# The end of attention and the start of the gated layer: a new plan of loads and preparing steps, part of it on GpSimd, and two tiles turned by TensorE

## The chip, the cores and the metric

The kernel runs on one core of a Trainium2 chip, as one program. The metric is the device time of one execution in microseconds. Before the change it is 778.28 us, the median of three runs (777.83 to 778.59).

## The reference, cut to what matters

Four batches of eight heads over 576 positions, head size 64; then a gated layer over the 2304 tokens, 512 wide inside and out, 1536 in the middle.

```python
scores = q @ k.T / sqrt(64) + bias                    # bias: a small network of the positions, per head
attn = exp(scores - max(scores)); attn = attn / (attn.sum(-1) + 1e-9)
x = (attn @ v)                                        # [4, 8, 576, 64] -> [2304, 512]
out = (sigmoid(x @ w_gate) * (x @ w_val)) @ w_out     # w_* come as float64 pairs of 32-bit words
```

## The kernel before, in words

It has three stages. The first builds the position bias (up to about 116 us). The second is attention, the third the gated layer (`Moe`).

**Attention.** There are 16 units, one for each pair of heads and batch, the batch running fastest: units 12 to 15 are the last pair of heads with batches 0 to 3. A unit has nine steps, numbered through as `n`; `score` (L633, L622) makes the scores `sc` on TensorE for two steps at a time, one for each head h, `soft` takes the bias and the row minimum on VectorE (L649) and the exponential on ScalarE (L654), which leaves `en`, 128 x 576. Two steps later `turn` (L673 to L686) transposes `en` into `at`, in two fp16 pieces, high and low. Head 0 and the ninth step go through TensorE: four 128 x 128 transposes into `pt`, the high piece on ScalarE, the low one on VectorE (`split`, L563, L564). The steps in `CROSS` (1, 3, 5, 7: all of head 1) go another way: GpSimd makes the two pieces `cr` (L531, L672), and a transposing DMA from SyncE's queue (L673) brings them into `at`, due `XLAG` = 2 steps later. `products` (L738) multiplies `at` with the values, in two halves of 14 pieces of two matmuls each, the second half of the columns after the first; `FILL` says how many pieces follow each step, and they belong to the unit before. After the last step two halves of the last unit remain. `tail` turns the ninth tile's last 64 columns, `normal` the row sums.

**Around the last units.** From unit 12 on, `extra(n)` runs at the end of each step and does what `PLAN` names, with n counted from unit 12's first step: `l0` loads 128 rows of `x` (piece 0 of four) of token chunk 0, `r0` the reciprocal sums of these rows, each `x0` is one of the steps of `prep_x` (nothing, the product with the reciprocals on VectorE, a high piece on ScalarE, a low piece on VectorE), `s` stages the next weight block from HBM, `w0` is the next step of weight block 0 (high piece on ScalarE, low piece on VectorE), `t` loads ScalarE's sigmoid table. Capital letters are chunk 1. What is left is done by `START[0]` ahead of the layer's first matmul, `START[1]` and `START[2]` behind the first and second pair. The order on an engine is not only that of the code: a scheduler may pull a step ahead, as the rows below show.

**The gated layer.** `ORDER` walks over pairs of a chunk (A: 0, B: 1) and one of 12 blocks of 128 middle columns: 24 matmuls of `gates` (L985) into `pg` and `pu`, then nine of `outs` (L1009) for the pair before. The blocks' weights are split into two pieces, those of blocks 3 and up also narrowed from float64, on VectorE and ScalarE, by `convert`, whose calls stand among the pairs. Engines run their instructions in order; SyncE's DMA queue too, so a load that waits holds those behind it.

Of the kernel before, what the change touches and what calls it, by code (L numbers as in the profile page):

```python
# [10 lines left out]
F32 = mybir.dt.float32  # L11
# [5 lines left out]
ALU = mybir.AluOpType  # L17
# [6 lines left out]
HF = S // 2  # L24
NCH = S // 64
FILL = (0, 7, 0, 7, 0, 7, 0, 7, 0)
ENB = 11
WM = 6
LAG, WSTEP, VSTEP, TAIL = 2, 2, (3, 5), 3
# [15 lines left out]
PRE = lambda f, z: f < 3  # L45
ORDER = "A0 A1 B0 A2 B1 A3 B2 A4 B3 A5 B4 A6 B5 A7 B6 A8 B7 A9 B8 A10 A11 B9 B10 B11"
CONV = (2, 1)
START = 'x0 x2 w3 x2 X0 s w0 w4 R1 w3 X0 w5 R2 X1 w4 w5 X2 w2 X1 L3 s X2 X1 X1', 'R3 s X2 s s X2 s', 'X3 X3 X3 X3'
PLAN = {
# [3 lines left out]
RAWS = 11  # L53
SLOTS = (12, 17)
ETILES, XTILES, XVARS = (7, 8), 10, 10
# [461 lines left out]
def attention(tc, att, q, k, v, biases, biasL, ident, xs, rs, sizes, extra):  # L517
# [41 lines left out]
    def half(ap):  # L559
        return ap.rearrange("p (a b) -> p a b", a=2)  # L560

    def split(hi, lo, ps):
        nc.scalar.activation(out=hi, in_=ps, func=AF.Copy, scale=float(2.0 ** UP))  # L563
        return lambda: nc.vector.scalar_tensor_tensor(out=lo, in0=ps, scalar=float(2.0 ** UP), in1=hi, op0=ALU.mult, op1=ALU.subtract)  # L564

    def pool_split(hi, lo, src):
        copy(hi, src)
# [90 lines left out]
    def turn(n):  # L658

        u, s = divmod(n, 9)  # L660
        p, b = units[u]
        if s == 0:
            state[u][1] = atp.tile([128, 2, 9, S], F16, name="at")
        sm, at, ens = state[u]
        h, it = TURN[s] if s < 8 else (0, 4)
        en = ens[4 * h + it if s < 8 else 8]
        i = slice(128 * it, 128 * it + 128)
        if s in CROSS:
            t = crp.tile([128, 2 * S], F16, name="cr")
            copy(t[:, 0:S], en)  # L670
            for a, z in ((640, slice(0, 512)), (S, slice(512, S))):
                nc.gpsimd.tensor_tensor(out=t[:, a:a + z.stop - z.start], in0=en[:, z], in1=t[:, z], op=ALU.subtract)  # L672
            crossed.append((n + LAG + XLAG, lambda: nc.sync.dma_start_transpose(out=at[:, h, :, i], in_=t)))  # L673
            return []
        after = []
        pt = ps_t.tile([128, 4, 128], F32, name="pt")
        for J in range(4):
            nc.tensor.transpose(pt[:, J], en[:, 128 * J:128 * J + 128], ident)  # L678
        if s == 8:
            return [split(at[:, h, 0:4, 512:576], at[:, h, 5:9, 512:576], pt[:, :, 64 * h:64 * h + 64]) for h in range(2)]  # L680
        after.append(split(at[:, h, 0:4, i], at[:, h, 5:9, i], pt))
        if it == 3:
            pt = ps_t.tile([128, 4, 128], F32, name="pt")
            for e in range(4):
                nc.tensor.transpose(pt[0:64, e], ens[4 * h + e][:, 512:576], ident)
            after.append(split(at[0:64, h, 4, 0:512], at[64:128, h, 4, 0:512], pt[0:64].rearrange("p e i -> p (e i)")))  # L686
        return after

    def tail(u):
# [60 lines left out]
    with tc.manual_schedule():  # L750
        work = iter(())
        after, late, due, loads = [], [], [], []
        for n in range(9 * NU + LAG + 1):
# [25 lines left out]
                inverse()  # L779
            if s == WSTEP and 0 < u < NU:  # L780
                work = products(u - 1)
            if n == 9 * NU + LAG - 1:
                work = products(u - 1)
            for _ in range(FILL[s] if n < 9 * NU else 14 if n < 9 * NU + LAG else 0):
                f = next(work, None)
                if f:
                    f()
# [3 lines left out]
                after.append(lower_v(u, VSTEP.index(s - 2)))  # L791
            if s == 8 and u + 1 < NU:
                loads.append(lambda z=u + 1: load_v(z))
            extra(n)
        for f in after + late:
            f()
        for f in work:
# [6 lines left out]
class Moe:  # L804
# [43 lines left out]

    def early(self, stack):

        self.open(stack, "right", sig=1, xin=3, xrec=2, x=4, wfirst=6)

    def ahead(self, n):
        self.do(PLAN.get(n, ""))
# [31 lines left out]

    def load_x(self, c, kc, eng=None):
        ts = slice(self.T * c, self.T * c + self.T)
        t = self.pools["xin"].tile([128, 2, self.T], F32, name="xin")
        (eng or self.nc.sync).dma_start(out=t[:, 0], in_=self.xs[128 * kc:128 * kc + 128, ts])  # L890
        return t

    def load_r(self, c, kc, eng=None):
# [5 lines left out]

    def prep_x(self, c, t, r, hi, lo, kc):  # L900
        nc = self.nc
        x = t[:, 0]

        return [lambda: None,
                lambda: nc.vector.tensor_tensor(out=x, in0=x, in1=r, op=ALU.mult),
                lambda: nc.scalar.activation(out=hi[:, kc], in_=x, func=AF.Copy),
                lambda: nc.vector.tensor_tensor(out=lo[:, kc], in0=x, in1=hi[:, kc].bitcast(F32), op=ALU.subtract)]

    def stage(self, eng=None):
        n = self.staged  # L910
# [12 lines left out]
    def begin(self):  # L923
# [11 lines left out]
        def upper():  # L935
            p = self.pools["wfirst" if n < 3 or (z == 2 and n > 5) else "wa"]
            t = p.tile([128, 2, 4, 128], F32R, tag="w", name=f"w{z}_{f}")
            self.wts[b] = t[:, 0], t[:, 1], t
            nc.scalar.activation(out=t[:, 0], in_=m, func=AF.Copy)
            if self.squares is None:  # L940
                self.unsized.append((f, z, t))
            else:
                self.size(f, z, t, t[:, 1])
# [70 lines left out]
    def store(self, c, t):  # L1014
        po = self.po.pop((c, t))
        if t == 2:
            ob = self.pools["xin"].tile([128, 2, self.T], F32, name="xin").rearrange("p s t -> p (s t)")[:, 0:DM]
        else:
            ob = self.pools["ob"].tile([128, DM], F32, name="ob")
        self.nc.scalar.activation(out=ob, in_=po, func=AF.Copy, **({"scale": self.un[c // 2][1]} if c > 1 else {}))  # L1020
# [335 lines left out]
```

## Time and profile before

| | us |
|---|---|
| runs, median (lowest to highest) | 778.28 (777.83 to 778.59) |
| the profiled execution, its own time | 779.37 |
| its span, first to last instruction | 777.6 |

| engine | busy us | share of the span |
|---|---|---|
| TensorE matmul (PE) | 729.3 | 94% |
| VectorE (DVE) | 632.7 | 81% |
| ScalarE (ACT) | 549.0 | 71% |
| GpSimd (POOL) | 325.3 | 42% |

Shares are means over stages that differ, so the stretches below are read one by one. Engines have the names in brackets, PEld is TensorE's weight load, SPq and ACTq are the DMA queues of SyncE and ScalarE. `x12` behind a name is a count. In a timeline row the brackets hold the time the engine was idle before the row and what ended it. PEclk is the share of full clock that TensorE was granted, 1.00 being 2.4 GHz.

### The profile page before, as it was taken

To read this page: it belongs to the slowest core of one execution; us is meant where nothing else is said; L and a number is where in the kernel's file an instruction comes from. 1 tells how busy PE (TensorE), PEld (TensorE's weight loads), DVE (VectorE), ACT (ScalarE), POOL (GpSimd) and SP (SyncE) were. 2 spreads that over 40 slices of the span, in tenths; PEclk is the share of its full clock that TensorE was granted. 3 is DMA by queue.
4 is the path that set the end of the run, shared out by engine and by line. 5 is a ranking of instruction groups with operands and counts; after the bars stand their busy time and mean duration, and the time that the engine had idled before them with its cause. 6 is when DMAs were issued, how large, how long until landed. Compare 5 with 4: busy or idle time off the path is not lost.

```text
span 777.6 us, 17819 instructions
## 1 busy us (share of the span) xinstructions
PE 729.3 (94%) x6695; PEld 536.0 (69%) x6695; DVE 632.7 (81%) x1342; ACT 549.0 (71%) x1190; POOL 325.3 (42%) x416
## 2 busy tenths in 40 slices
PE   7998978999999998878999999999999999999997
PEld 4888866777777776657998999955555555555553
DVE  6788989999999998864698988879989886777662
ACT  5887839888898987857576665677667667566653
POOL 2243448999899897640000000124524340543200
PEclk9999999999999999988999999999999999999999
DMA  6487415898887999776787633334421213412102
GB/s 205 137 203 184 137 60 121 168 199 175 169 194 158 196 203 206 162 152 216 251 277 229 219 118 109 126 123 139 156 83 56 81 55 109 149 45 78 55 1 81
DMA packets 130965, 112.43 MB, mean 145 GB/s; under 512 B 81216, under 2 KB 101824, under 8 KB 130880
## 3 DMA queue, kind: packets, MB, share of 16 engines
q1 hardware_dynamic: 126848, 105.74, 49.8%
q0 software_dynamic: 2112, 2.62, 2.3%
q10 hardware_dynamic: 1920, 2.95, 1.1%
q8 instruction: 52, 0.85, 0.5%
q14 instruction: 33, 0.27, 0.1%
HBM read 76.08 MB, written 18.95 MB: 122 GB/s over the span
## 4 chain that ended last, share of the span: by engine, by line
PE 59%; DVE 11%; ACT 9%; issue 4%; DMA 2%; POOL 0%; SPq 0%; ACTq 0%; DVEq 0%
PE po L1009 16%; PE pg L1157 10%; PE pu L1157 7%; PE pg L985 6%; PE pu L985 6%; PE acc L738 5%; PE sc L633 4%; PE pt L678 3%; DVE en L649 3%; ACT at L563 3%; ACT en L654 3%; DVE at L564 2%; PE sc L622 1%; DVE wv L1126 1%; DVE xt L1041 1%
## 5 line engine op out<-in xcount | busy, mean ns | idle before, releaser
L1115 POOL TENSOR_TENSOR ws<-wm 128x256 f32<-128x256 f32 x44 | 43.7, 994 | 298.7 <-DMA xt<-xs 161.2
L1157 PEld LDWEIGHTS <-wv 128*128 128x128 f16 x1008 | 98.1, 98 | 83.1 <-issue 8.1
L654 ACT ACTIVATE en<-en,mn 128x576 f32<-128x576 f32 x144 | 110.7, 774 | 17.8 <-DVE mn L649 16.0
L1157 PE MATMUL pg<-xq,wv 128*128 128x384 f16 x576 | 109.3, 326 | 2.1 <-ACT c L1183 1.7
L649 DVE CUSTOM_DVE_ANT_0 en<-sc,bias 128x576 f32<-128x576 f32 x128 | 91.8, 754 | 11.2 <-PE sc L633 10.2
L672 POOL TENSOR_TENSOR cr<-en,cr 128x512 f16<-128x512 f32 (+1 forms) x128 | 92.4, 744 | 5.3
L1009 PE MATMUL po<-wo,gh 128*128 128x512 f16 x288 | 85.7, 379 | 0.0
L1157 PE MATMUL pu<-xq,wv 128*128 128x384 f16 x432 | 82.0, 326 | 1.6 <-DVE c L1163 1.6
L564 DVE SCALAR_TENSOR_TENSOR at<-pt,at 128x512 f16<-128x512 f32 (+3 forms) x128 | 70.1, 568 | 13.6 <-ACT at L563 12.1
L633 PE MATMUL sc<-k,part 64*128 64x288 f32 x768 | 74.8, 313 | 3.6 <-DVE mn L649 1.9
L738 PE MATMUL acc<-at,vv 128*64 128x288 f16 x868 | 68.8, 296 | 9.0 <-DMA at<-cr 6.2
L1163 DVE TENSOR_TENSOR c<-pu,c 128x384 f32<-128x384 f32 x72 | 39.9, 555 | 41.8 <-PE pu L1157 27.2
L633 PEld LDWEIGHTS sc<-k,part 64*128 64x128 f32 x768 | 58.8, 187 | 18.0 <-issue 10.9
L427 PE MATMUL bps<-cfs,ind 128*128 128x64 bf16 x1458 | 67.5, 193 | 3.8 <-DVE bias L443 1.9
L408 ACT ACTIVATE ind<-y 128x576 bf16<-128x576 f32 x100 | 62.4, 651 | 10.8 <-PE y L403 8.0
L563 ACT ACTIVATE at<-pt 128x512 f16<-128x512 f32 (+3 forms) x128 | 60.4, 496 | 10.5 <-PE pt L678 10.0
L738 PEld LDWEIGHTS <-vv 128*64 128x64 f16 x896 | 49.8, 112 | 24.7 <-issue 20.7
L427 PEld LDWEIGHTS <-ind 128*128 128x128 bf16 x1458 | 58.7, 98 | 9.8 <-issue 3.1
L1175 ACT ACTIVATE gh<-c 128x384 f16<-128x384 f32 x48 | 25.1, 522 | 54.6 <-DVE c L1173 52.9
L678 PE MATMUL pt<-ident,en 128*128 128x128 f32 x320 | 51.8, 285 | 9.9 <-ACT en L654 5.1
L985 PE MATMUL pg<-xhi,w 128*128 128x384 f32 x192 | 54.2, 341 | 2.4 <-ACT g L994 2.4
L1009 PE MATMUL po<-wo,gl 128*128 128x512 f16 x144 | 54.6, 379 | 0.0
(179 smaller groups left out, 1672.1 us busy)
## 6 DMA issues: line engine op xcount, KB each, us to landing
wm<-scratch SPq DMA_DIRECT2D x48, 256.0 KB
scratch<-wm SPq DMA_DIRECT2D x27, 256.0 KB
wo<-scratch SPq DMA_DIRECT2D x24, 256.0 KB
qr<-in_q_dram SPq DMA_DIRECT2D x16, 320.0 KB
vr<-in_v_dram SPq DMA_DIRECT2D x16, 320.0 KB
kr<-in_k_dram SPq DMA_DIRECT2D x16, 288.0 KB
xs<-xe SPq DMA_DIRECT2D x16, 288.0 KB
xrec<-rs SPq DMA_DIRECT2D x48, 96.0 KB
```

The source lines that it names most:

```text
L427: nc.tensor.matmul(out=o, lhsT=st, rhs=cfs[:, part], start=(part == 0), stop=(part == 2))
L563: nc.scalar.activation(out=hi, in_=ps, func=AF.Copy, scale=float(2.0 ** UP))
L564: return lambda: nc.vector.scalar_tensor_tensor(out=lo, in0=ps, scalar=float(2.0 ** UP), in1=hi, op0=ALU.mult, op1=ALU.subtract)
L633: nc.tensor.matmul(out=pair[h][:, e, 0:HF], lhsT=qs[rows, l, 128 * it:128 * it + 128], rhs=ks[rows, r, HF * e:HF * e + HF], start=(i == 0) ...
L649: nc.vector.tensor_tensor_reduce(out=half(en), in0=ps[:, :, 0:HF], in1=half(nbias), scale=-0.125, scalar=3.0e38, op0=ALU.add, op1=ALU.min, ...
L654: nc.scalar.activation(out=en, in_=en, func=AF.Exp, bias=mn, scale=-1.0, accum_out=sm)
L672: nc.gpsimd.tensor_tensor(out=t[:, a:a + z.stop - z.start], in0=en[:, z], in1=t[:, z], op=ALU.subtract)
L678: nc.tensor.transpose(pt[:, J], en[:, 128 * J:128 * J + 128], ident)
L738: nc.tensor.matmul(out=acc[D * h:D * h + D, 0:HF], lhsT=vv[:, h, J, z], rhs=at[:, h, y, cs], start=(i == 0), stop=(i == len(mms) - 1))
L985: self.nc.tensor.matmul(out=(pg, pu)[z], lhsT=l, rhs=r, start=(kc == 0 and i == 0), stop=(kc == 3 and i == 2))
L1009: self.nc.tensor.matmul(out=po, lhsT=l[:, tt], rhs=r, start=(first and i == 0), stop=(last and i == 2))
L1157: nc.tensor.matmul(out=p, lhsT=W[i][:, l, at + kc], rhs=V[b][:, r, kc], start=(new and n == 0), stop=(n == 5), skip_group_check=not new)
```

## The change

Five things change together. `PLAN` and `START` are rewritten: all four pieces of chunk 0 and three of chunk 1, and the low pieces of weight blocks 0 and 1, are finished or nearly so within attention; the loads are spread differently; `START` shrinks to steps of weight blocks 2 to 5 and the last piece of chunk 1. Three pieces of chunk 1 (`OWN_X`) are prepared on GpSimd alone. In the last unit the steps 5 and 7 are no longer crossed but turned by TensorE, ScalarE and VectorE as head 0's are, without the scale 2^14 that head 1 already carries. `LASTF` replaces `FILL` in the last unit: unit 14's products end within it, and the first half of unit 15's follow its last step. `prep_x` loses its empty step. Pools: `xin` has four buffers for three, each smaller, `xrec` three for two; the squares of weight blocks 3 to 5 are taken later.

```diff
+LASTF = (14, 7, 0, 7, 0, 7, 0, 14, 0)
-START = 'x0 x2 w3 x2 X0 s w0 w4 R1 w3 X0 w5 R2 X1 w4 w5 X2 w2 X1 L3 s X2 X1 X1', 'R3 s X2 s s X2 s', 'X3 X3 X3 X3'
+START = 's w2 w3 w3 w2 X3 w4 s X3 X3 w4', 's s s s w5 w5', ''
 PLAN = {
...
-    18: "w0", 19: "s", 20: "l3", 21: "w1 x2", 22: "L0 r3", 24: "s", 26: "w2 x3", 27: "R0 w1", 31: "x3 L2", 32: "x3",
-    33: "x3", 35: "X0", 36: "s", 37: "t X0"}
...
+    34: "X2 R3", 35: "X2 s", 36: "w0 w1 t s", 37: "w2"}
+OWN_X = (1, 0), (1, 1), (1, 2)
...
-    def split(hi, lo, ps):
+    def split(hi, lo, ps, up=UP):
...
-        if s in CROSS:
+        if s in CROSS and not (u == NU - 1 and s > 3):
...
-        after.append(split(at[:, h, 0:4, i], at[:, h, 5:9, i], pt))
-        if it == 3:
+        up = 0 if h else UP
+        after.append(split(at[:, h, 0:4, i], at[:, h, 5:9, i], pt, up))
+        if it == 3 or h:
+            e0 = it if h else 0
+            c = slice(128 * e0, 128 * it + 128)
             pt = ps_t.tile([128, 4, 128], F32, name="pt")
-            for e in range(4):
+            for e in range(e0, it + 1):
...
-            if n == 9 * NU + LAG - 1:
+            if n == 9 * NU:
                 work = products(u - 1)
-            for _ in range(FILL[s] if n < 9 * NU else 14 if n < 9 * NU + LAG else 0):
+            if n >= 9 * NU:
+                extra(n)
+            for _ in range((FILL if u < NU - 1 else LASTF)[s] if n <= 9 * NU else 0):
...
-        self.open(stack, "right", sig=1, xin=3, xrec=2, x=4, wfirst=6)
+        self.open(stack, "right", sig=1, xin=4, xrec=3, x=4, wfirst=6)
...
+        x = t[:, 0:self.T]
+        own = (c, kc) in OWN_X
+        eng = nc.gpsimd if own else nc.vector
+        def upper():
+            if own:
+                eng.tensor_scalar(out=hi[:, kc], in0=x, scalar1=1.0, scalar2=1.0, op0=ALU.mult, op1=ALU.mult)
+            else:
+                nc.scalar.activation(out=hi[:, kc], in_=x, func=AF.Copy)
+        return [lambda: eng.tensor_tensor(out=x, in0=x, in1=r, op=ALU.mult), upper,
+                lambda: eng.tensor_tensor(out=lo[:, kc], in0=x, in1=hi[:, kc].bitcast(F32), op=ALU.subtract)]
...
-            if self.squares is None:
+            if self.squares is None or n < 6:
```

TensorE at the last step of the last unit, before: the scores of step 8, the turn of step 6 with head 0's four last 64-column parts, and then products of unit 14.

```order
L622 MATMUL sc<-k,part 128x288 x6
L678 MATMUL pt<-ident,en 128x128 x4
L685 MATMUL pt<-ident,en 64x128 x4
L738 LDWEIGHTS vv
L738 MATMUL acc<-at,vv 64x288
```

The same place after it:

```order
L624 MATMUL sc<-k,part 128x288 x6
L680 MATMUL pt<-ident,en 128x128 x4
L690 MATMUL pt<-ident,en 64x128 x4
L680 MATMUL pt<-ident,en 128x128 x4
L690 MATMUL pt<-ident,en 64x128
L743 LDWEIGHTS vv
L743 MATMUL acc<-at,vv 64x288
```

The turn of step 7 (the second group of four transposes and its one 64-column part) has come between, and the products behind it are now the first half of unit 15's.

VectorE in unit 14, at steps 4 and 5, before (`mn` is what ScalarE's exponential of step 5 waits for):

```order
L649 ISA en,mn<-sc,bias_73 128x576
L649 ISA mn 128x1
L649 ISA en,mn<-sc,bias_73 128x576
L649 ISA mn 128x1
L907 TENSOR_TENSOR xlo<-xin,xhi 128x384
L948 TENSOR_TENSOR w_0_6853<-ww,w_0_6853 128x512
L653 TENSOR_SCALAR mn<-mn 128x1
L564 SCALAR_TENSOR_TENSOR at<-pt,at 64x2x64
L564 SCALAR_TENSOR_TENSOR at<-pt,at 128x4x128
```

The same place after it:

```order
L651 ISA en,mn<-sc,bias_73 128x576
L651 ISA mn 128x1
L651 ISA en,mn<-sc,bias_73 128x576
L651 ISA mn 128x1
L655 TENSOR_SCALAR mn<-mn 128x1
L566 SCALAR_TENSOR_TENSOR at<-pt,at 64x2x64
L566 SCALAR_TENSOR_TENSOR at<-pt,at 128x4x128
```

The low pieces of an `x` tile and of weight block 0 no longer stand ahead of the minimum `mn` of step 5. The `x` piece's now comes at step 1 of this unit, weight block 0's with block 1's behind the last unit's sums.

GpSimd at the end of the last unit, with tile numbers, before: the crossings of steps 5 and 7, then two fills.

```order
L531 TENSOR_SCALAR cr_7312<-en_7238 128x576
L672 TENSOR_TENSOR cr_7312<-en_7238,cr_7312 128x512
L672 TENSOR_TENSOR cr_7312<-en_7238,cr_7312 128x64
L531 TENSOR_SCALAR cr_7361<-en_7297 128x576
L672 TENSOR_TENSOR cr_7361<-en_7297,cr_7361 128x512
L672 TENSOR_TENSOR cr_7361<-en_7297,cr_7361 128x64
L865 MEMSET sig_7426 128x1
L1259 MEMSET ones_7526 128x128
```

After, from the second own `x` piece on:

```order
L920 TENSOR_TENSOR xin_6862<-xin_6862,xrec_6953 128x384
L533 TENSOR_SCALAR cr_7201<-en_7118 128x576
L674 TENSOR_TENSOR cr_7201<-en_7118,cr_7201 128x512
L674 TENSOR_TENSOR cr_7201<-en_7118,cr_7201 128x64
L916 TENSOR_SCALAR xhi_6823<-xin_6862 128x384
L921 TENSOR_TENSOR xlo_6824<-xin_6862,xhi_6823 128x384
L533 TENSOR_SCALAR cr_7264<-en_7182 128x576
L674 TENSOR_TENSOR cr_7264<-en_7182,cr_7264 128x512
L674 TENSOR_TENSOR cr_7264<-en_7182,cr_7264 128x64
L920 TENSOR_TENSOR xin_7074<-xin_7074,xrec_7163 128x384
L916 TENSOR_SCALAR xhi_6823<-xin_7074 128x384
L921 TENSOR_TENSOR xlo_6824<-xin_7074,xhi_6823 128x384
```

The crossings of steps 5 and 7 are gone. The crossing of step 1 stands between the parts of the second own piece, and that of step 3 now comes behind the second piece's last two parts and ahead of the whole third piece.

## Rows read from the trace of the kernel before

**Rows 1.** The stretches: length, busy us of each engine, PEclk, DMA share, GB/s.
```profile
256.20:269.90 13.70, 13.08 (x142) 10.19 (x140) 12.69 (x35) 12.07 (x32) 12.56 (x17) 1.00 0.82 174
290.80:307.30 16.50, 13.57 (x138) 10.30 (x138) 14.12 (x39) 13.12 (x34) 12.66 (x17) 1.00 0.94 228
307.30:325.40 18.10, 14.95 (x139) 11.39 (x138) 16.21 (x39) 13.60 (x35) 15.30 (x19) 0.91 0.78 170
325.40:339.70 14.30, 13.27 (x141) 10.08 (x141) 13.41 (x38) 13.36 (x34) 7.01 (x11) 1.00 0.51 121
339.70:353.70 14.00, 8.20 (x77) 5.97 (x76) 3.66 (x10) 5.26 (x12) 1.60 (x4) 0.76 0.82 152
360.50:366.40 5.90, 5.86 (x25) 5.86 (x26) 1.70 (x4) 3.86 (x10) 0.00 (x0) 0.71 0.79 266
366.40:505.60 139.20, 138.71 (x729) 128.70 (x729) 117.88 (x234) 88.53 (x197) 3.02 (x4) 1.00 0.58 194
```

**Rows 2.** TensorE's timeline: start us, us, what, count, [idle before, releaser].
```profile
297.76 1.02 PE L738 MATMUL acc<-at,vv 128*64 128x288 f16 x13 [1.55 <-DMA at<-cr]
320.41 0.63 PE L678 MATMUL pt<-ident,en 128*128 128x128 f32 x4 [2.32 <-ACT rt L702]
320.97 1.89 PE L738 MATMUL acc<-at,vv 128*64 128x288 f16 x14
338.24 0.60 PE L678 MATMUL pt<-ident,en 128*128 128x128 f32 x4
339.67 1.05 PE L738 MATMUL acc<-at,vv 128*64 128x288 f16 x14
346.77 3.52 PE L738 MATMUL acc<-at,vv 128*64 128x288 f16 x27 [4.67 <-DMA at<-cr]
351.89 1.90 PE L738 MATMUL sc<-at,vv 128*64 128x288 f16 x27 [0.65 <-DMA at<-cr]
353.72 0.44 PE L985 MATMUL pg<-xhi,w 128*128 128x384 f32 x1
360.54 0.44 PE L985 MATMUL pg<-xhi,w 128*128 128x384 f32 x1 [2.38 <-ACT g L994]
```

**Rows 3.** The chain of waits: start us, us, what; gates of two pairs.
```profile
360.54 3.06 PE pg L985 x12
363.60 2.96 PE pu L985 x12
374.89 2.08 PE pg L985 x12
```

**Rows 4.** The timeline of SyncE's DMA queue, the last two crossed tiles.
```profile
343.45 1.29 SPq L673 DMA_TRANSPOSE at<-cr  x1
345.98 2.42 SPq L673 DMA_TRANSPOSE at<-cr  x1
```

**Rows 5.** The timeline of ScalarE between attention and the first layer pair.
```profile
350.80 1.28 ACT L866 ACT_TABLE_LOAD   x1
359.59 0.52 ACT L906 ACTIVATE xhi<-xin 128x384 fp32r<-128x384 f32 x1 [1.83 <-DVE xin L905]
```

**Rows 6.** The timeline of VectorE in the last units.
```profile
297.83 0.56 DVE L905 TENSOR_TENSOR xin<-xin,xrec 128x384 f32<-128x384 f32 x1
317.52 1.64 DVE L948 TENSOR_TENSOR w<-ww,w 128x512 fp32r<-128x512 f32 x1
329.04 0.63 DVE L948 TENSOR_TENSOR w<-ww,w 128x512 fp32r<-128x512 f32 x1
335.31 0.68 DVE L564 SCALAR_TENSOR_TENSOR at<-pt,at 128x512 f16<-128x512 f32 x1
```

**Rows 7.** The timeline of GpSimd in the last two units.
```profile
309.99 1.42 POOL L568 TENSOR_TENSOR k<-kr,k 128x576 fp32r<-128x576 f32 x1
317.27 2.06 POOL L672 TENSOR_TENSOR cr<-en,cr 128x512 f16<-128x512 f32 x2
332.62 0.67 POOL L531 TENSOR_SCALAR cr<-en 128x576 f16<-128x576 f32 x1 [0.66 <-ACT en L654]
```

More of the change, by code (lines that the diff above doesn't have):

```diff
@@ L560, in half @@
         return ap.rearrange("p (a b) -> p a b", a=2)
-    def split(hi, lo, ps):
-        nc.scalar.activation(out=hi, in_=ps, func=AF.Copy, scale=float(2.0 ** UP))
-        return lambda: nc.vector.scalar_tensor_tensor(out=lo, in0=ps, scalar=float(2.0 ** UP), in1=hi, op0=ALU.mult, op1=ALU.subtract)
+    def split(hi, lo, ps, up=UP):
+        nc.scalar.activation(out=hi, in_=ps, func=AF.Copy, scale=float(2.0 ** up))
+        return lambda: nc.vector.scalar_tensor_tensor(out=lo, in0=ps, scalar=float(2.0 ** up), in1=hi, op0=ALU.mult, op1=ALU.subtract)
     def pool_split(hi, lo, src):
@@ L680, in turn @@
             return [split(at[:, h, 0:4, 512:576], at[:, h, 5:9, 512:576], pt[:, :, 64 * h:64 * h + 64]) for h in range(2)]
-        after.append(split(at[:, h, 0:4, i], at[:, h, 5:9, i], pt))
-        if it == 3:
+        up = 0 if h else UP
[3 more added lines that the diff above has]
+            c = slice(128 * e0, 128 * it + 128)
             pt = ps_t.tile([128, 4, 128], F32, name="pt")
-            for e in range(4):
+            for e in range(e0, it + 1):
                 nc.tensor.transpose(pt[0:64, e], ens[4 * h + e][:, 512:576], ident)
-            after.append(split(at[0:64, h, 4, 0:512], at[64:128, h, 4, 0:512], pt[0:64].rearrange("p e i -> p (e i)")))
+            after.append(split(at[0:64, h, 4, c], at[64:128, h, 4, c], pt[0:64].rearrange("p e i -> p (e i)")[:, c], up))
         return after
@@ L793, in attention @@
                 loads.append(lambda z=u + 1: load_v(z))
-            extra(n)
+            if n < 9 * NU:
+                extra(n)
         for f in after + late:
@@ L888, in load_x @@
         ts = slice(self.T * c, self.T * c + self.T)
-        t = self.pools["xin"].tile([128, 2, self.T], F32, name="xin")
-        (eng or self.nc.sync).dma_start(out=t[:, 0], in_=self.xs[128 * kc:128 * kc + 128, ts])
+        t = self.pools["xin"].tile([128, DM], F32, name="xin")
+        (eng or self.nc.sync).dma_start(out=t[:, 0:self.T], in_=self.xs[128 * kc:128 * kc + 128, ts])
         return t
@@ L901, in prep_x @@
         nc = self.nc
[L902 to L907, printed above, removed]
+        x = t[:, 0:self.T]
[8 more added lines that the diff above has]
+                lambda: eng.tensor_tensor(out=lo[:, kc], in0=x, in1=hi[:, kc].bitcast(F32), op=ALU.subtract)]
     def stage(self, eng=None):
@@ L1016, in store @@
         if t == 2:
-            ob = self.pools["xin"].tile([128, 2, self.T], F32, name="xin").rearrange("p s t -> p (s t)")[:, 0:DM]
+            ob = self.pools["xin"].tile([128, DM], F32, name="xin")
         else:
```

3 rows, old and new, of the table PLAN are left out of this document.

## The prediction

> **What bounds the kernel now.** I read the stretches first, cut where the units of attention begin, then TensorE's timeline and the chain, then the engine that ended each wait. A unit runs in 13.7 us when nothing disturbs it, with TensorE busy for 13.08 of them: TensorE is the bound, but VectorE (12.69) and GpSimd (12.56) have about one microsecond to spare, so what is put on them in such a unit is soon late [rows 1]. The units in which the layer's preparation runs are longer: unit 13 takes 16.5 us, unit 14 18.1, unit 15 14.3, which is 2.8, 4.4 and 0.6 too much [rows 1]. The reader sees in TensorE's timeline what ended the idle times: in unit 13 a transposing DMA (1.55 us), in unit 14 a wait of 2.32 us for ScalarE, behind which 14 product matmuls take 1.89 us instead of 1.05; the granted clock of that unit is 0.91 [rows 1, 2]. ScalarE was late there because VectorE did a weight block's low piece of 1.64 us ahead of the row minimum that ScalarE needs [rows 6].
>
> Then comes the hole that the change is about. Between the products at 339.67 and the layer's first matmul at 353.72 lie 14.05 us, in which TensorE is busy for some 8 of 14 and the clock is 0.76 [rows 1, 2]. It waits 4.67 us for the crossed tile of step 5 and 0.65 us for that of step 7, and the 27 matmuls behind the first wait run at half clock, 3.52 us where the same 27 take 1.90 at full clock [rows 2]. The first pair of the layer runs at once, but the second waits 2.38 us for ScalarE, which waited 1.83 us for VectorE's product of an `x` tile [rows 2, 5], and then runs its gates partly at 1.2 GHz: 3.06 and 2.96 us where a later pair takes 2.08 [rows 3]; the granted clock there is 0.71. From 366.4 to 505.6 TensorE is busy for 138.71 of 139.20 us [rows 1], so a stage that starts earlier should end earlier by as much, unless its supply fails.
>
> **The change part by part.**
>
> *Units 13 and 14.* In unit 13 VectorE gets five `x` steps of 0.56 us where it had four [rows 6], and SyncE one weight load less ahead of the transposing DMAs, but the reciprocals of piece 2 now go ahead of the values' load. I leave its excess at 2.8 us, between 1.25 (the DMA wait of 1.55 gone) and 4.4 (as unit 14 was). Of the three `x` and weight steps that VectorE had in unit 14 only one low piece of 0.56 us stays, and it fits the spare microsecond. The wait of 2.32 and the slow products (0.84) go, and the lesser losses that hung on the slow clock with them: 4.4 becomes 0.5, between 0 and 1.2. That is a gain of 3.9 us.
>
> *Unit 15.* TensorE gets two tiles to turn: 2 x 4 transposes at 0.60 us for four, and two smaller ones at no more than 0.15 each, 1.5 us; and the 14 matmuls (1.05 us) that completed unit 14's products after the last step now stand before it [rows 2]. The unit becomes 14.3 + 2.55 = 16.85 us, a loss of 2.55. ScalarE and VectorE each get two more large pieces (0.68 us on VectorE [rows 6]) and two quarter-width ones; beside a unit that is 2.55 us longer VectorE's 1.7 to 2 us are covered. What would be late first if they are not is the exponential of step 8.
>
> *GpSimd.* An own `x` piece is two tensor_tensor operations and a copy over 384 columns. From 1.42 us and 0.67 us for 576 columns I scale to 0.95, 0.45 and 0.95, that is 2.35 us, three times 7 us; two crossings go. In unit 15 GpSimd was busy for 7.01 us of 14.3 [rows 1, 7], so there is room. But a wait is new: the crossing of step 3 stands behind two parts of the second own piece, and behind it in SyncE's queue stand the unit's sums, the last reciprocals and the loads of weight blocks 3 and 4. In the kernel before, the crossing of step 3 began at 332.62, 7.2 us into the unit. With 1.4 us ahead of it and 2.7 of its own it is done 11.3 us in; a crossed tile reached TensorE 3.32 us after its DMA was issued (343.45 to 346.77) [rows 2, 4], so it is there at 14.6. The products that want it start at 16.85: 2.2 us to spare, and cost nothing.
>
> On that new use of GpSimd the row of unit 14 speaks against the change: there VectorE's 1.64 us piece (0.63 elsewhere) and the two subtractions of GpSimd's crossing (2.06 us) ran at the same moment [rows 6, 7]. The Trainium skill has a rule for it (SBUF — State Buffer, Who interferes with whom): a VectorE operation with two SBUF inputs and a GpSimd operation that reads SBUF take a shared read interface in turn, and the second to start stands until the first is done. The trace agrees with its 1.64 us. By that rule each meeting would cost up to one GpSimd operation. It is the first rival below. In my sum it has no part, since VectorE keeps only two `x` steps of this kind in unit 15.
>
> *The hole.* No DMA is left on the path: behind the last step TensorE does the first half (28 matmuls, 1.97 us by the 27 in 1.90), the last tile's four transposes (0.60), two small ones (0.30) and the second half (1.97), together 4.85 us [rows 2]. The second half needs the last tile's pieces from ScalarE, and ScalarE now loads its sigmoid table, 1.28 us [rows 5], ahead of these pieces. No row shows that wait; it lies between 0 and the 2.32 us of the longest wait for ScalarE above. I take 1.3, the table load, its nearest row. So 14.05 us become 6.15, a gain of 7.9.
>
> *The first two pairs.* Both weight blocks and all of chunk 0 are ready before the first pair. The last `x` piece of chunk 1 still has its three steps ahead of the first pair's sigmoid, but its loads are issued two steps before the end of attention and no longer behind it, so the wait of 2.38 goes (between 0 and 2.38 stays; I take 0, since 1.83 of it was the wait for that product). With no idle time ahead, the second pair's gates run at full clock: 3.06 + 2.96 - 2 x 2.08 = 1.86.
>
> *Sum.* 3.9 - 2.55 + 7.9 + 2.38 + 1.86 = 13.5 us. The profiled execution had 779.37 us, 1.77 of them outside its span of 777.6; it would come to 765.9. The median is 1.09 lower than that execution, so the forecast for the median is 778.28 - 13.5 = **764.8 us**.
>
> **The rivals.**
>
> *GpSimd and VectorE hold each other up, or the crossing of step 3 is late.* For it speaks the meeting at 317.5 us, which cost VectorE 1.0 us [rows 6]; in unit 15 two VectorE steps can meet GpSimd's, 2 us, and if TensorE then waits long enough to lose its clock, as it did behind the 2.32 us wait, the products add about 1.9. Against it, the 2.2 us to spare. Time: 766.8 to 768.7.
>
> *TensorE waits for the last tile as long as it did for ScalarE in unit 14.* Then 2.32 instead of 1.3, the second half at half clock (3.52 for 1.90), and the second pair's 1.86 not regained: 1.0 + 1.6 + 1.86 = 4.5 us, 769.3. For it, the table load on ScalarE's way; against it, the 1.55 us wait in unit 13, behind which 13 matmuls took 1.02 us, full clock [rows 2].
>
> *The gain is given back in the layer.* If the weights' loads set the pace of the layer's first third, its end does not move: about 778. For it, a DMA share of 0.79 in the second pair; against it, 0.58 over the next 139 us, with TensorE idle for only 0.5 us of them [rows 1].
>
> *Slower than before: the second pair's weights are late.* Weight blocks 3 and 4 are now loaded in the last unit, one of them into the place that block 0's low piece frees behind the last sums. Issued an estimated 1.5 us behind the last step (two low pieces of 0.63 us and the sums stand ahead [rows 6]) and landing as late as the slowest crossed tile (345.98 to 351.89, 5.9 us) [rows 2, 4], they are there 7.4 us behind it, while the second pair starts 6.15 + 4.4 = 10.5 us behind it. The 4.4 is from 353.72 to the wait of 2.38 us ahead of 360.54 [rows 2]. From 3 us later on each microsecond counts; to be slower than before they must be 16.5 us late, and then every pair behind them is. Time: 780 or more. Nothing in the rows takes that long.
>
> **How the numbers follow.** The forecast has a chance of 0.70, with its own range from 761 (unit 13's DMA wait gone, no wait for the last tile) to 768 (unit 13 1.6 us worse, unit 14 at 1.2, part of the 2.38 left). The first rival has 0.12, the second 0.10, the given-back gain 0.04, the slower case 0.04. From 760 to 771 us leaves out about 0.15: the last two cases, both first rivals at once, and little below. A measurement of this kernel can tell 0.2%, some 1.6 us, from no change: faster than that has 0.92, within it 0.04, slower 0.04.
>
> **What would show it.** Right: unit 14 under 14.5 us; no idle time of TensorE put down to a transposing DMA behind the last step; the layer's first matmul about 6 us behind the start of unit 15's first products; no wait between the first two pairs; 2.1 us for each of the second pair's two gate groups. Wrong: a unit 13 or 14 as long as before, a wait for `cr` at unit 15's first products, a clock under 0.9 between attention and the second pair, or idle time of TensorE for weights in the layer's first third.

## The result and the profile after

The changed kernel takes 769.54 us, the median of four runs (768.97 to 771.19), beside 778.12 us before on the same chip (777.83 to 778.59): a ratio of 0.9893, with a 95% interval of 0.9875 to 0.991. The forecast was 764.8 us and the range 760 to 771. The kernel is faster, by 8.6 us where 13.5 were forecast. The profiled execution had 769.07 us and a span of 767.2, which is 10.4 less than the span before.

The stretches of the changed kernel, cut where a unit's first score matmuls begin: units 13, 14 and 15, the hole, the second pair's gates, the layer's first third (columns as in [rows 1]).

```profile
290.70:307.58 16.88, 14.55 (x139) 10.68 (x138) 15.10 (x39) 13.47 (x34) 13.34 (x17) 1.00 0.97 220
307.58:321.93 14.35, 13.41 (x139) 10.30 (x138) 13.65 (x37) 12.60 (x33) 12.93 (x17) 1.00 0.88 198
321.93:340.50 18.57, 16.45 (x163) 12.32 (x163) 16.75 (x41) 15.42 (x40) 13.78 (x20) 1.00 0.71 180
340.50:346.83 6.33, 5.42 (x63) 3.92 (x62) 4.74 (x11) 5.20 (x14) 0.00 (x0) 1.00 0.37 120
351.39:355.80 4.41, 4.41 (x25) 4.41 (x26) 1.43 (x3) 2.05 (x5) 0.00 (x0) 1.00 1.03 349
355.80:494.90 139.10, 138.60 (x727) 128.26 (x726) 117.13 (x233) 91.77 (x207) 2.78 (x3) 1.00 0.58 191
```

The reader is to see three things. The granted clock is 1.00 in every row, where it had been 0.91, 0.76 and 0.71 in three rows of before [rows 1]. The last row is as long as its counterpart, 139.1 us for 139.2 [rows 1], so what was gained ahead of it was kept. And unit 15 takes 18.57 us, where the prediction had 16.85.

TensorE's timeline of the changed kernel, from the last unit's end to the second pair, without the matmuls in between.

```profile
339.32 0.60 PE L690 MATMUL pt<-ident,en 128*64 128x128 f32 x4 [0.99 <-DVE at L566]
340.50 1.91 PE L743 MATMUL acc<-at,vv 128*64 128x288 f16 x28
343.57 0.30 PE L697 MATMUL pt<-ident,en 128*64 128x128 f32 x1 [0.57 <-DVE at L566]
344.09 0.56 PE L743 MATMUL sc<-at,vv 128*64 128x288 f16 x2
344.82 2.08 PE L743 MATMUL sc<-at,vv 128*64 128x288 f16 x26 [0.18 <-DVE at L566]
346.83 0.44 PE L999 MATMUL pg<-xhi,w 128*128 128x384 f32 x1
351.39 0.44 PE L999 MATMUL pg<-xhi,w 128*128 128x384 f32 x1
```

None of the waits is put down to a transposing DMA, against 4.67 and 0.65 us before, and the second pair starts without the wait of 2.38 us [rows 2]. Its gates take 2.37 and 2.08 us in the chain, for 3.06 and 2.96 [rows 3].

```profile
351.39 2.37 PE pg L999 x12
353.76 2.08 PE pu L999 x12
```

VectorE in unit 15 of the changed kernel, the three pieces of work that took longer than the same work elsewhere:

```profile
325.22 0.89 DVE L724 TENSOR_TENSOR sm<-sm,small 128x9 f32<-128x9 f32 x1
326.28 1.19 DVE L920 TENSOR_TENSOR xin<-xin,xrec 128x384 f32<-128x384 f32 x1
329.59 0.80 DVE L921 TENSOR_TENSOR xlo<-xin,xhi 128x384 fp32r<-128x384 f32 x1
341.34 0.17 DVE L724 TENSOR_TENSOR sm<-sm,small 128x9 f32<-128x9 f32 x1
```

The sums take 0.89 us where the same sums take 0.17 in the hole (last row), the `x` product 1.19 for 0.56 [rows 6]. GpSimd is at work on the own `x` pieces in just these moments:

```profile
325.08 1.01 POOL L921 TENSOR_TENSOR xlo<-xin,xhi 128x384 fp32r<-128x384 f32 x1
326.05 1.00 POOL L920 TENSOR_TENSOR xin<-xin,xrec 128x384 f32<-128x384 f32 x1
327.02 0.98 POOL L533 TENSOR_SCALAR cr<-en 128x576 f16<-128x576 f32 x1
329.47 0.51 POOL L916 TENSOR_SCALAR xhi<-xin 128x384 fp32r<-128x384 f32 x1
330.07 1.18 POOL L921 TENSOR_TENSOR xlo<-xin,xhi 128x384 fp32r<-128x384 f32 x1
```

Each of the three VectorE operations starts while one of GpSimd's runs. The first two meet the operations at 325.08 and 326.05, the third meets the one-input copy at 329.47. At its start 0.87, 0.77 and 0.39 us of GpSimd's operation are left, and it ends 0.02, 0.42 and 0.41 us behind GpSimd's end: what it loses is about the rest of the operation that it met. So some 1.6 us of VectorE's 16.75 are time in which it is held up. That looks like the whole answer, 18.57 less 16.85. The experiments show that it is only half of one. That such meetings have a price could be read before the change: there the same sums took 0.51 us in unit 13 and 0.71 in unit 14, against 0.16 in unit 15, at a moment when GpSimd was idle.

```profile
310.73 0.71 DVE L719 TENSOR_TENSOR sm<-sm,small 128x9 f32<-128x9 f32 x1
328.71 0.16 DVE L719 TENSOR_TENSOR sm<-sm,small 128x9 f32<-128x9 f32 x1
```

### The profile page after: what moved, and what is told of

It reads as the page before. It is cut to its first block, busy times and chain, and to the rows that moved or that the text cites. A ratio compares the mean times of both kernels' runs of the same rounds, so it can differ in the third digit from the quotient of the medians.

```text
span 767.2 us, 17839 instructions
## 1 busy us (share of the span) xinstructions
PE 728.1 (95%) x6705; PEld 534.6 (70%) x6705; DVE 630.8 (82%) x1340; ACT 549.5 (72%) x1191; POOL 328.3 (43%) x419
## 4 chain that ended last, share of the span: by engine, by line
PE 62%; DVE 11%; ACT 7%; issue 3%; DMA 3%; SPq 0%; POOL 0%; ACTq 0%; DVEq 0%
PE po L1023 17%; PE pg L1171 10%; PE pu L1171 8%; PE pg L999 6%; PE pu L999 6%; PE acc L743 5%; PE sc L635 4%; DVE en L651 4%; PE pt L680 3%; ACT at L565 3%; DVE at L566 2%; ACT en L656 2%; PE sc L624 1%; DMA vr<-in_v_dram 1%; DMA xrec<-rs 1%
## 5 line engine op out<-in xcount | busy, mean ns | idle before, releaser
L674 POOL TENSOR_TENSOR cr<-en,cr 128x512 f16<-128x512 f32 x124 | 89.3, 742 | 5.2
L635 PE MATMUL sc<-k,part 64*128 64x288 f32 x768 | 77.7, 316 | 5.1 <-DVE mn L651 3.1
L566 DVE SCALAR_TENSOR_TENSOR at<-pt,at 128x512 f16<-128x512 f32 (+3 forms) x132 | 72.1, 565 | 5.4 <-ACT at L565 3.7
L743 PE MATMUL acc<-at,vv 128*64 128x288 f16 x868 | 65.7, 288 | 2.7 <-ACT xe L747 0.9
L743 PEld LDWEIGHTS <-vv 128*64 128x64 f16 x896 | 48.1, 109 | 17.2 <-issue 14.6
```

The costliest lines, as they stand in the source:

```text
L635: nc.tensor.matmul(out=pair[h][:, e, 0:HF], lhsT=qs[rows, l, 128 * it:128 * it + 128], rhs=ks[rows, r, HF * e:HF * e + HF], start=(i == 0) ...
L743: nc.tensor.matmul(out=acc[D * h:D * h + D, 0:HF], lhsT=vv[:, h, J, z], rhs=at[:, h, y, cs], start=(i == 0), stop=(i == len(mms) - 1))
```

## The experiments

All ratios are to the kernel before, timed on the same chip; stage lengths are from each kernel's one profiled execution, from the start of unit 13, 14 or 15 to the next. Of the ratios' intervals only those of the turned tiles alone, of the crossing put back, and of two late kernels (chunk 0's last piece on GpSimd, and all three edits) lie clear of the changed kernel's, so what the other edits are worth is read from stage lengths. How far one profile can be trusted for that differs by stage. Unit 15 took 18.57 us in the changed kernel, 18.62 and 18.55 in the two whose only edits are the earlier loads and these with the later table, and 18.88 with the later table alone; unit 13 moved by more than a microsecond in two executions, as told below.

**Chunk 1's `x` back on VectorE and ScalarE.**

```diff
-OWN_X = (1, 0), (1, 1), (1, 2)
+OWN_X = ()
```

> The changed kernel (769.5 us), with chunk 1's three x pieces back on VectorE and ScalarE. VectorE gets six operations of 0.56 us (3.3 us) in the last unit, ScalarE three of 0.51, GpSimd loses 7.7. Theory A (VectorE sets the pace of unit 15, and part of its 16.8 busy us there is time in which GpSimd's reads hold it up, 0.7 us on the sums, 0.6 and 0.25 on the x steps): unit 15 grows by 3.3 less some 1.6 given back, from 18.6 to 20.3 us, and the sums and x steps shrink to 0.2 to 0.56 us; 771.2 us. Rival B (VectorE sets the pace, and being held up costs nothing): 21.9 us, 772.8. Rival C (the prediction's: VectorE is covered): no change.

Measured: 771.39 us, ratio 0.9901 (0.9883 to 0.992), no different from the changed kernel by the intervals. Its profile tells more.

```profile
321.07:342.90 21.83, 18.16 (x163) 13.38 (x163) 18.12 (x48) 17.29 (x43) 6.96 (x11) 0.92 0.66 162
```

Unit 15 is 21.83 us, rival B's number, but in part by luck: the granted clock is 0.92, and behind a wait of 1.04 us eight transposes take 1.97 us that take 1.06 in the changed kernel. No theory had that. VectorE's sums are at 0.16 and the `x` steps at 0.55 us, as theory A had it, but the time was not given back: VectorE now waits 2.13 us for TensorE's piece of the values, and ScalarE 0.8 for the values' load. That it is GpSimd that holds VectorE up is shown; what it costs is not.

**The turned tiles alone, on the plan of before.** The diffs of `split`, `turn`, the products' order and LASTF are applied to the kernel before; PLAN, START, the buffers and `prep_x` stay.

> The kernel before with one part of the change alone: the last two crossed tiles turned by TensorE, and the products' new order; the plan of x and weight steps, the buffers and the engines of x stay. Units 13 and 14 as before (16.5 and 18.1 us). Unit 15 gets longer by 2.55, the 5.3 us of waits for crossed tiles go. If that alone brings the hole's gain, the layer's first matmul comes 5.3 us earlier, 772.9 us. If the second pair then waits for chunk 1's x, which stays behind SyncE, ScalarE and VectorE as it was, the wait of 2.38 grows and 2 us or so are left: 776. I expect the second.

Measured: 776.99 us, ratio 0.9973 (0.9957 to 0.999), as the second theory had it. From the start of unit 13 to the layer's first matmul are 59.68 us, for 63.02 before: the hole gives 8.3 us, a unit 14 of 16.6 in this execution 1.5, and unit 15 takes 6.8 of it back. The second pair then waits longer than before, and part of its gates runs at half pace. TensorE, and ScalarE in unit 15:

```profile
357.13 0.69 PE L992 MATMUL pg<-xhi,w 128*128 128x384 f32 x1 [2.73 <-ACT g L1001]
```

```profile
332.94 0.56 ACT L604 ACTIVATE vv<-vr,vup 128x320 f16<-128x320 f32 x1 [2.47 <-DMA vr<-in_v_dram]
```

So the turned tiles alone bring little; what the plan brings without them is the next run. The second row is the find: unit 15 took 21.02 us here (granted clock 0.92), with VectorE busy for only 15.99, and ScalarE waited 2.47 us for the load of the unit's own values.

**Steps 5 and 7 crossed again.**

```diff
-        if s in CROSS and not (u == NU - 1 and s > 3):
+        if s in CROSS:
```

> The changed kernel with steps 5 and 7 of the last unit crossed on GpSimd and turned by DMA again; all else as changed. GpSimd gets some 5 us more in unit 15 (13.8 to about 18 of 18.6), TensorE loses 1.5 us, VectorE and ScalarE two large pieces each. If VectorE sets the pace of unit 15 (theories A and B), the unit gets shorter by 1.5 to 2 us; then TensorE waits 4 to 6 us for the crossed tiles and loses its clock behind them, as before: 773 to 776 us. If those waits were due to the old place of the x work in the queues, little is lost: 768 to 770.

Measured: 774.46 us, ratio 0.9947 (0.9928 to 0.9966). Unit 15 falls to 16.18 us, and the hole becomes 13.1:

```profile
343.50 3.52 PE L743 MATMUL acc<-at,vv 128*64 128x288 f16 x27 [5.04 <-DMA at<-cr]
```

That is the wait of before, 4.67 us, with the same 27 matmuls at 3.52 [rows 2]: with the turned tiles taken back it is there again, so it is they that remove it. (GpSimd's own `x` pieces also end the crossing of step 5 later in the unit, 14.6 us in for 12.3 before, so the run does not show what the new loads and steps would do to this wait without them.) The turned tiles cost 2.4 us in unit 15 (18.57 less 16.18) and save 6.8 in the hole.

**GpSimd's two-input operations replaced by copies.**

```diff
+        def plain(out):
+            eng.tensor_scalar(out=out, in0=x, scalar1=1.0, scalar2=1.0, op0=ALU.mult, op1=ALU.mult)
...
+        if own:
+            return [lambda: plain(x), upper, lambda: plain(lo[:, kc])]
```

> The changed kernel, where GpSimd's six x operations with two inputs (1.00 us each) are replaced by copies with one input (0.51 us): chunk 1's first three x pieces are not multiplied by the reciprocals and their low pieces are not remainders. VectorE's work is the same to the instruction. Theory A (the holding up by GpSimd's two-input reads costs time): the sums (0.89 us), the x product (1.19) and the low piece (0.80) in unit 15 get shorter by some 1 us together, and the unit by as much: 17.6 us, 768.5. Rival B (only VectorE's own work counts): no row of VectorE shorter, unit 15 18.6 us, 769.5.

Measured: 768.91 us, ratio 0.9868 (0.9847 to 0.9889). The rows of VectorE did what theory A says, and unit 15 what rival B says:

```profile
322.94:341.46 18.52, 15.82 (x164) 11.96 (x163) 15.29 (x41) 15.28 (x40) 10.64 (x19) 1.00 0.72 181
```

```profile
326.23 0.26 DVE L724 TENSOR_TENSOR sm<-sm,small 128x9 f32<-128x9 f32 x1
326.64 0.54 DVE L925 TENSOR_TENSOR xin<-xin,xrec 128x384 f32<-128x384 f32 x1
333.31 0.69 DVE L566 SCALAR_TENSOR_TENSOR at<-pt,at 128x512 f16<-128x512 f32 x1 [0.84 <-ACT at L565]
336.81 0.69 DVE L566 SCALAR_TENSOR_TENSOR at<-pt,at 128x512 f16<-128x512 f32 x1 [0.81 <-ACT at L565]
```

The sums still meet a copy, but only 0.24 us of it are left when they start, and they take 0.26. The product meets nothing. The low piece starts first (329.47), and here it is GpSimd that loses: its copy beside it takes 0.89 us for 0.51.

```profile
325.96 0.51 POOL L921 TENSOR_SCALAR xin<-xin 128x384 f32<-128x384 f32 x1
329.50 0.89 POOL L916 TENSOR_SCALAR xhi<-xin 128x384 fp32r<-128x384 f32 x1
```

VectorE is busy 1.46 us less, 15.29 for 16.75, and stands idle for it, behind ScalarE, which in this run waits 1.0 us for the values' load (0.5 in the changed kernel). Neither theory was right: a second limit lies just behind the first. Its cause is in SyncE's queue. Before the change, where unit 15 began at 325.42, and after it, where it began at 321.93:

```profile
328.56 0.52 SPq L553 DMA_DIRECT2D vr<-in_v_dram  x1
329.18 1.36 SPq L673 DMA_TRANSPOSE at<-cr  x1
330.64 0.63 SPq L744 DMA_DIRECT2D xs<-xe  x1
```

```profile
322.91 1.55 SPq L675 DMA_TRANSPOSE at<-cr  x1
326.59 0.33 SPq L749 DMA_DIRECT2D xs<-xe  x1
327.02 1.17 SPq L555 DMA_DIRECT2D vr<-in_v_dram  x1
```

LASTF completes unit 13's products at the start of unit 15, so the store of their outputs stands ahead of the values' load. The queue is idle from 324.5 to 326.59 us, where it waits for ScalarE's copy of these outputs, which ends at 326.57, and the load is issued 5.1 us into the unit instead of 3.1. The run with the turned tiles alone, which has LASTF but not the new plan, has the same order: store at 327.80, load at 328.25, 5.0 us into its unit 15.

```profile
326.18 0.39 ACT L747 ACTIVATE xe<-acc 128x288 f32<-128x288 f32 x1
```

**The values' loads one step earlier.**

```diff
-            if s == 8 and u + 1 < NU:
+            if s == (7 if u > NU - 5 else 8) and u + 1 < NU:
                 loads.append(lambda z=u + 1: load_v(z))
```

> The changed kernel, with the loads of the values of the last four units issued one step earlier on SyncE; no other engine's order differs. The runs so far leave two theories of the last unit's extra 1.7 us. Theory V (found in the copies' run: VectorE became 1.46 us freer and the unit stayed 18.5): the values' load stands behind the store of the outputs of two units back, which waits for ScalarE, so it is issued 5.1 us into the unit (before: 3.1), and ScalarE waits for it 1.1 us in unit 13 and 0.5 in unit 15. Then these waits go: unit 13 15.8 us instead of 16.9, unit 15 18.1, since VectorE is the next to be late there; about 768.0. Theory D (VectorE alone sets the pace): the waits go and both units stay as long; 769.5.

Measured: 769.13 us, ratio 0.988 (0.9859 to 0.9902). The waits for the values are gone, and units 13 and 15 are as long as in the changed kernel, 16.89 and 18.62 us: theory D's outcome, and theory V's size for this edit alone was wrong. VectorE, as busy as in the changed kernel (16.71 us for 16.75), is now late there by itself.

```profile
321.41:340.03 18.62, 16.46 (x163) 12.31 (x162) 16.71 (x41) 15.47 (x40) 13.83 (x20) 1.00 0.77 187
```

**Both: copies, and the values earlier.** The two diffs together.

> The run with copies in place of GpSimd's two-input x operations (it leaves out the multiplication and the remainders of chunk 1's first three pieces), with the earlier values' loads as well. Theory V (two things, each enough: VectorE held up by GpSimd, and the values late): with both gone unit 15 falls from 18.5 to 17.0, and unit 13 to 15.8; about 766.5. If neither matters (theory E: TensorE's and ScalarE's own work makes the 18.5), unit 15 stays within 0.3 us of 18.5.

Measured: 767.91 us, ratio 0.9862 (0.9846 to 0.9879).

```profile
321.80:339.17 17.37, 16.02 (x163) 12.16 (x162) 15.36 (x41) 15.17 (x40) 10.72 (x19) 1.00 0.73 180
```

Unit 15 falls to 17.37 us. Taken away alone, the one limit gives 0.05 us and the other nothing; together they give 1.2. Theory V holds for unit 15, in its second form. The medians do not tell these kernels apart: the ratios are 0.9868, 0.988 and 0.9862, with intervals that overlap. Unit 13 stays at 16.87, where 15.8 was expected; the next run bears on what holds it.

**Low pieces one step later, with the earlier loads.**

```diff
-    ... 9: "x0 r2", 10: "x0", 12: "x1", 13: "x1", 14: "x1 L0", 16: "x2 s", 17: "x2 R0", 18: "x2 L1",
+    ... 9: "x0 r2", 11: "x0", 12: "x1", 13: "x1", 14: "L0", 15: "x1", 16: "x2 s", 17: "x2 R0", 18: "L1", 19: "x2",
```

> The changed kernel, with the earlier values' loads, and with the low pieces of chunk 0's first three x pieces one step later each, so that VectorE does not stand for ScalarE's high piece (1.5 us of such waits in unit 13). If VectorE's standing is on the path of unit 13, the unit falls to between 14.6 and 15.8 us, unit 14 stays within 0.5; 767 us. If another engine is late then, no more than the earlier loads alone.

Measured: 768.6 us, ratio 0.9865 (0.9841 to 0.9889). Unit 13 falls to 15.59 us, as expected: VectorE's standing for ScalarE's high pieces (1.5 us in the changed kernel) was on the path. Then unit 15 gives it back, at 20.15 us:

```profile
329.45 1.02 PE L743 MATMUL acc<-at,vv 128*64 128x288 f16 x13 [3.06 <-DMA at<-cr]
```

The DMA of the tile that it waits for was issued 33.9 us behind the start of unit 13, where the run with the earlier loads alone had issued it at 32.5. TensorE was earlier, SyncE's queue was later. Nearly all of the 1.4 us went at one store, which the queue took up 22.9 us behind that start in both runs. With the earlier loads alone, and here:

```profile
313.07 0.56 SPq L749 DMA_DIRECT2D xs<-xe  x1
```

```profile
314.04 1.93 SPq L749 DMA_DIRECT2D xs<-xe  x1
```

Why the store took longer here is open, so part of the 20.15 us may be this one execution.

**The sigmoid table later.**

```diff
-START = 's w2 w3 w3 w2 X3 w4 s X3 X3 w4', 's s s s w5 w5', ''
+START = 't s w2 w3 w3 w2 X3 w4 s X3 X3 w4', 's s s s w5 w5', ''
...
-    34: "X2 R3", 35: "X2 s", 36: "w0 w1 t s", 37: "w2"}
+    34: "X2 R3", 35: "X2 s", 36: "w0 w1 s", 37: "w2"}
```

> The changed kernel, with ScalarE's load of the sigmoid table moved behind attention's last pieces, ahead of the first pair's weight steps. The prediction put 1.3 us of the hole down to that load. Theory F (it is on the path to the last tile's pieces): the second half of the last products starts 0.8 to 1.3 us earlier, the hole falls from 6.3 to 5.0 to 5.5 us, and the first pair's sigmoid is not later: 768.4. Theory G (the last tile waits for VectorE's pieces or TensorE's own work): no change in the hole, and the table load may delay the second pair; 769.5 or more.

Measured: 769.3 us, ratio 0.9882 (0.9862 to 0.9903). The hole is 5.85 us for 6.33, so the load's price in it is 0.5 us and not the 1.3 that I took. The wait of 0.57 us for VectorE's last piece stays as it was; the wait of 0.18 is gone, and the last 28 matmuls take 2.4 us instead of 2.7. In this execution unit 13 was 18.1 us, because the values landed late:

```profile
300.97 0.56 ACT L605 ACTIVATE vv<-vr,vup 128x320 f16<-128x320 f32 x1 [2.70 <-DMA vr<-in_v_dram]
```

**Earlier loads and chunk 0's last piece on GpSimd.**

```diff
-OWN_X = (1, 0), (1, 1), (1, 2)
+OWN_X = (0, 3), (1, 0), (1, 1), (1, 2)
```

> The changed kernel with the earlier values' loads, and with chunk 0's last x piece on GpSimd too. It takes two of VectorE's operations (0.55 us each, held up to 1.19 and 0.80) out of unit 15 and puts some 2.5 us on GpSimd (13.8 to 16.3 busy us). Theory H (two limits in unit 15, each enough by itself: VectorE held up, and the values late; the copies' run with early values had both gone and 17.4 us): unit 15 falls from 18.6 to between 17.4 and 18.0; about 768. Rival J (GpSimd becomes the limit: the crossing of step 3 comes 2.5 us later, and the last products wait for its tile): the hole grows by 1 to 2.5 us, 769.5 to 771.

Measured: 767.65 us, ratio 0.9855 (0.984 to 0.987), which is below the interval of the changed kernel. Of the kernels that leave no work out none is clearly better (all three edits together, below, come to 0.9854): it is 0.4% or some 3 us below the changed one by the ratios, 1.9 us by the medians.

```profile
291.08:308.96 17.88, 15.64 (x139) 11.96 (x138) 16.10 (x41) 13.50 (x34) 14.25 (x18) 0.90 0.95 210
308.96:322.71 13.75, 13.01 (x139) 10.12 (x138) 12.68 (x35) 12.53 (x33) 12.02 (x16) 1.00 0.83 204
322.71:339.66 16.95, 15.71 (x163) 11.98 (x163) 14.48 (x39) 14.75 (x39) 15.56 (x23) 1.00 0.70 165
```

Unit 15 takes 16.95 us, close to the prediction's own 16.85, and 16.96 in the run of all three edits. VectorE is 2.3 us less busy than in the changed kernel, the sums are at 0.28 us, GpSimd's 15.56 of 16.95 still fit and the hole stays at 6.3; rival J is out. (Unit 13 was 17.88 us in this execution, at a granted clock of 0.90, so the gain of the kernel does not come from there.)

**Earlier loads and the later table; then all three edits.**

> The changed kernel with the earlier values' loads and the sigmoid table loaded behind attention's last pieces. In the run with the later table alone the hole was 5.85 us instead of 6.33, but unit 13 was 18.1 us instead of 16.9, with a wait of 2.7 us for the values. If that wait was the values' load and nothing of the table's (theory V2), unit 13 is 16.9 here, without a wait for the values, and the hole 5.9: 768.8. If the table's move made unit 13 longer, it is 18 again.

> All three edits together: earlier values' loads, chunk 0's last x piece on GpSimd, the sigmoid table later. The kernel that the runs so far point to. If each gain stands (unit 15 by 0.6 to 1.2 us, the hole by 0.5): 767.8. If GpSimd is the limit with the extra piece, no better than the run without it.

Measured: 768.19 us, ratio 0.9863 (0.9848 to 0.9877), and 768.28 us, ratio 0.9854 (0.9837 to 0.9871). In the first, unit 13 is 16.88 us with no wait for the values, so the 18.1 had been that load's landing. In the second the layer starts 54.0 us behind the start of unit 13 (56.1 in the changed kernel), but it waits behind the second pair's gates, for a piece of the first pair from VectorE:

```profile
356.88 0.50 PE L1023 MATMUL po<-w,gl 128*128 128x512 f32 x1 [1.53 <-DVE gl L1011]
```

The wait there is 0.67 us in the first of the two and 0.32 in the run with the later table alone; without the later table there is none, in the changed kernel and in the one before this. So what the later table saves in the hole it costs there.

**Later low pieces with the extra GpSimd piece, and one weight load moved back.** The diffs of the last `x` piece, the earlier loads and the later low pieces, and:

```diff
-    16: "x2 s", ... 23: "l3"
+    16: "x2", ... 22: "s", 23: "l3"
```

> The kernel with earlier values' loads and chunk 0's last x piece on GpSimd, with the low pieces of chunk 0's first pieces one step later as well, and the load of the second weight block six steps later on SyncE, behind three of the transposing DMAs that come after it now. With the low pieces later and nothing else, unit 13 fell to 15.6 us and unit 15's first products then waited 3.06 us for a transposing DMA: SyncE's DMAs went on at their old times. Theory K (SyncE's queue sets when those tiles come): unit 13 again 15.6, and the weight load's place gives back some 0.5 of the wait: products wait 2 to 3 us, about the time of the kernel without this edit, 767.7. If the wait came from that one load, it goes: 766.2.

Measured: 769.6 us, ratio 0.9881 (0.9857 to 0.9905), at theory K's end or above it. Unit 13 is 15.42 us, and unit 15 20.71:

```profile
328.82 1.84 PE L743 MATMUL acc<-at,vv 128*64 128x288 f16 x13 [2.21 <-DMA at<-cr]
```

The wait is 0.85 us shorter, with one load less ahead, and the 13 matmuls behind it take 1.84 us instead of 1.02 (the unit's granted clock is 0.92, where it was 1.00 behind the longer wait of 3.06). The one load was not the only cause. The DMA waited for was issued 32.0 us behind the start of unit 13, and 32.5 in the kernel without the later low pieces, where TensorE came 2 us later and found its tile there. Here the tile came 5.2 us behind its issue (323.58 to 328.82), there within 4.5. So TensorE is earlier than the tile can be, by its place in the queue, by its time on the way or by both; no run made the queue shorter or the way quicker, and which of them is the third limit is open.

## Why the prediction was right in direction and 3 us off in its terms

The terms, in the profiled executions: 13.5 us were forecast and 10.4 of the span went.

- *Unit 13*, forecast unchanged at 16.5 us: 16.88. The DMA wait of 1.55 us [rows 2] went to 0.19, and VectorE's 1.5 us of standing for high pieces took its place: 0.4 short. ScalarE's wait for the values, 1.10 us, is not the reason. It was 1.17 before the change, and the unit stayed at 16.89 without it; with the standing gone as well it fell to 15.59. The prediction also named a unit 13 as long as before as a sign of being wrong, though its own sum left the unit unchanged: that sign could not tell anything.
- *Unit 14*, forecast 14.2: 14.35. The step was right, the clock is 1.00, the wait of 2.32 us is gone.
- *Unit 15*, forecast 16.85: 18.57. **This step failed**, 1.7 of the 3.1 us. The loss for TensorE was worked out well (17.37 us with the copies and the earlier loads, 16.95 with VectorE relieved of two more operations). What failed is the clause that VectorE's added work is covered by the longer unit. It had been added up at undisturbed prices, and it needs 1.6 us more since GpSimd reads at the same moments. I had given the Trainium skill's rule on just this (SBUF — State Buffer, Who interferes with whom: one of the two engines stands while the other holds the interface they share) no part in the sum, because only two `x` steps were left to VectorE. The trace agrees with the rule, in 0.72, 0.63 and 0.24 us for three operations, the sums among them, which I had not thought of as one that can be met, though the trace before shows them at 0.51 and 0.71 us. The first rival, which did count on such meetings, has one half: they alone keep the unit at 18.62 with the values early. But with VectorE's loss in them down to 0.1 us the unit stayed at 18.52. The other half is a move in SyncE's queue that the prediction did not follow: pulling unit 13's last products ahead puts their store before the values' load. Each of the two is enough, which three runs show: with the one taken away unit 15 is 18.52 us, with the other 18.62, with both 17.37.
- *The crossing of step 3*: right. It was done 11.5 us into the unit, for 11.3, and there is no wait for `cr` at the last products.
- *The hole*, forecast 6.15: 6.33, right in sum by two errors. The wait for the last tile is 0.57 and 0.18 us and not 1.3, and the last 28 matmuls take 2.74 us (344.09 to 346.83, the wait of 0.18 among them) and not 1.97. With the table later they take 2.44 (344.61 to 347.05), so 0.3 of it hangs on the table load; why the rest is slower at a granted clock of 1.00 I did not test. The second rival's half clock there did not come.
- *The two pairs and what follows*, forecast 4.24: 3.6 by what is left of the span. The wait of 2.38 us is gone, the gates gave 1.57 of 1.86 [rows 3]: the first group took 2.37 us and not 2.1.

The other part of the distance has nothing to do with the change's mechanism. I took 1.1 us off because before's profiled execution lay above its median; after's lies 0.5 below its own. So 3.2 us from terms (by the two executions' own times, 10.3 went) and 1.6 from executions make the 4.7 between 764.8 and 769.5.

The range holds the time, but not by the forecast's own account: 769.54 lies above the 768 up to which the forecast was to be right (its lower end, by the terms named there, is 762 rather than 761). It is nearest to the second rival's 769.3, and that is chance, since neither the long wait for the last tile nor the half clock behind it came.

The gain was not given back in the layer, and the second pair's weights were not late: the last two rivals fell with the 139.1 us row.

## What to carry to other kernels

A stage with three engines near their limit has limits in layers, and taking one away can show nothing: before a cost is called hidden, ask which wait is next, and test two removals together. When work is pulled forward, follow its stores through the DMA queue too, since a store that waits for its data holds every load behind it. Where two engines share operands' memory, add up their work at the prices of meetings that the trace already shows and not at the undisturbed ones.

## What was not expected of the hardware

VectorE's sums over 9 columns took 0.89 us beside a GpSimd operation with two inputs (1.01 us), and 0.17 alone; beside a one-input copy (0.51 us) they took 0.26. The price is not a fixed one, since it goes by what is left of the operation that is met: 0.87 and 0.24 us were left there. So a short operation can lose several times its own length, and a one-input copy on GpSimd holds VectorE up too (0.80 us for 0.56), only for less long. A load of the values took so long in one execution that ScalarE waited 2.70 us for it and in another 1.10, with the issue at the same place in the queue; a load issued on time can thus move a run by more than a microsecond. And the length of a wait alone did not tell what TensorE's clock did behind it: behind 3.06 us 13 matmuls took 1.02 us, behind 2.21 us 13 matmuls took 1.84.
